# Convolution and gated product, start-up: bands without filling matmuls, two column rests in one product, weight copies ahead of loads, block 4 later

## The chip, the cores and the metric

One core of a Trainium2 chip runs the kernel. The metric is the device time of one execution in microseconds; the lower the better. Times of the profile are counted from the start of the profiled span.

## The reference

```
x:       8 sequences x 3904 tokens x 192 channels, float32
weight:  8 heads x 7 taps; softmax over the taps of each head
conv:    out[b, s, h, :] = sum over k of softmax(weight)[h, k] * x[b, s - 6 + k, h, :]   (zeros ahead of a sequence)
a = conv @ w1   (192 -> 1024)
b = conv @ w2   (192 -> 1024)
out = ((a * b) @ w3) @ w_out   (1024 -> 1024 -> 192), float32
```

The kernel multiplies w3 by w_out once (`W_sb`, 1024 x 192) and applies that product to `a * b`.

## The kernel before

The 31232 tokens form two streams (`NS = 2`), the first four sequences and the last four. The partitions hold one stream in their lower half (64 rows) and the other in their upper half. A window is 64 rows of x, of which 58 are new tokens; windows are grouped into blocks of 6, 4, 8, 10, 8, then six of 36 and one of 20.

The convolution is done on PE (TensorE): for each head a 64 x 64 band matrix is the stationary operand and x of the block the moving one (`conv`, line 291). Four groups of bands (`band`, line 256) are built at the start, from products of a diagonal with the softmaxed taps (`cprod`, line 247, on DVE), each with 28 small matmuls, and copied out of PSUM by ACT (the first two) or DVE (the last two). Between two bands stands one filling matmul on zeros, 128 columns wide (`warm(1, 128)`, line 206); five fillers of 512 columns stand at the start, and two more before the bands.

The conv's result goes to SBUF as `convo` and must then be transposed into `xT` (channels on partitions). Blocks 0 to 4 are transposed by PE (`pe_transpose`, line 340; `joint_transposes` for block 1, line 489), the later ones through DRAM (`rows`) by DMA transposes that SP queues (line 360).

Tokens of each stream are worked on in rounds of 512. In each round `first_product` makes eight tiles (ft 0 to 7) of 128 features: per tile six matmuls for w1 (`wd[0]`) and six for w2 (`wd[1]`), 64 rows each, so that both streams run side by side; then ACT copies the first result to `asb` (line 386) and DVE multiplies it with the second into `abT` (line 387). Four pairs of PSUM banks (`pairs`, `banks()`, `drained()`) go round in the order in which they were given back. `second_product` (line 415) multiplies `abT` with `W_sb`. Rounds run in groups of four: their first products, then their second products with the convs of a later block between them.

Round 0 begins before all of its 512 columns are there: block 0 gives the first 348 (`EARLY`). Tiles 0 and 1 are made for these 348 columns, and then for the other 164, when block 1 has been transposed. Tiles 2 to 7 follow at full width, with the convs of blocks 2 and 3 between them.

The weights w1 and w2 come in four parts of 256 features: part 0 by SP into `wfirst`, parts 1 to 3 by POOL's queue into the lower 64 partitions (line 172), and POOL copies each part to the upper 64 (`copy_w`, line 193). Part 1 serves tiles 2 and 3, part 2 tiles 4 and 5, part 3 tiles 6 and 7. All of this stands in program order in POOL's queue together with the loads of x (`load_x`, line 120) and of w3 (line 441, in two halves, cast to bf16 in DRAM as `w3rows`). w3 is then transposed by 16 DMA transposes on SP's queue (line 445). POOL waits for the fourteenth of them with a copy of two elements (`pace`, line 539), and only then loads x of blocks 5 and 6. Where a sequence begins inside a block, POOL zeroes the rows ahead of it after the load (line 546).

Of the kernel before, what the change touches and what calls it, by code (L numbers as in the profile page):

```python
# [9 lines left out]
BF16 = mybir.dt.bfloat16  # L10
AX = mybir.AxisListType
ALU = mybir.AluOpType
# [4 lines left out]
def kernel(  # L17
# [53 lines left out]
    def banks():  # L71
        p = free.pop(0)
        return p, pairs[:, NS * p:NS * p + NS, :]
# [4 lines left out]
    def drained(p):  # L78
        assert p not in free
        free.append(p)  # L80
# [24 lines left out]
    def load_x(b, parts=(0, 1), between=()):  # L105
        between = list(between)
        tiles = xb_of.setdefault(b, [])
        zeros_of = zero_rows.setdefault(b, [])
        for i0, n in [v for e, v in enumerate(halves_of(b)) if e in parts]:
            xb = work.tile([128, n, D], BF16, tag="xb", bufs=5, name="xb")  # L110
            w = 0
            while w < n:
                i = i0 + w
                m = min(n - w, WB - i % WB)
                at_end = i + m == NWIN
                if at_end:
                    m -= 1
                if m:
                    for r in range(NS):
                        nc.gpsimd.dma_start(out=xb[Q * r:Q * r + Q, w:w + m, :],  # L120
                                            in_=x_spans(r, i, m))
                        if between:
                            between.pop(0)()
                if i % WB == 0:
                    zeros_of += [(xb, 0, w), (xb, 1, w)]
                w += m
                if at_end:
                    nc.gpsimd.memset(xb[Q:128, w, :], 0.0)
                    t = tok(NWIN - 1) - PAD
                    nc.gpsimd.dma_start(out=xb[0:Q, w, :], in_=x_rows[t:t + Q, :])  # L130
                    nc.gpsimd.dma_start(out=xb[Q:Q + PAD + LAST, w, :],
                                        in_=x_rows[TS + t:TS + t + PAD + LAST, :])
                    w += 1
            if len(halves_of(b)) == 1:
                tiles += [(xb, 0), (xb, SIZES[b] // 2)]
            else:
                tiles.append((xb, 0))
# [8 lines left out]
    pace = const.tile([1, 2], BF16)  # L146
    tiny = const.tile([128, 1], FP32)
    ones = const.tile([128, 1], BF16)
    zeros = const.tile([128, CH], BF16)
    half = const.tile([1, 3 * Q], BF16)  # L150
    ident = const.tile([128, 128], BF16)
    diag = const.tile([128, Q + PAD], BF16)
    nc.vector.memset(tiny, 0.0)
    nc.vector.memset(ones, 1.0)
    nc.vector.memset(zeros, 0.0)  # L155
    nc.vector.memset(xb0[:, 0, :], 0.0)
    nc.vector.memset(half, 0.0)
    nc.vector.memset(half[:, Q:2 * Q], 1.0)
# [10 lines left out]
    def load_w(part):  # L169
        cs = slice(WC[part], WC[part + 1])  # L170
        for i in range(2):
            nc.gpsimd.dma_start(out=wd[i][0:Q, :, cs], in_=w_rows[i][:, :, cs])  # L172
# [18 lines left out]
    def copy_w(part, i, f):  # L191
        cs = slice(WC[part], WC[part + 1])
        f(out=wd[i][Q:128, :, cs], in_=wd[i][0:Q, :, cs])  # L193
# [3 lines left out]
    load_w(2)  # L197
    load_x(2, between=[seq((copy_w, 1, i, nc.gpsimd.tensor_copy) for i in range(2))])
    load_w(3)
    load_x(3)  # L200
    load_x(4)

    def warm(n, cols=CH):
        p, t = banks()
        for j in range(n):
            nc.tensor.matmul(t[:, j % 2, 0:cols], zeros[:, 0:128], zeros[:, 0:cols],  # L206
                             start=True, stop=True)
        drained(p)

    warm(5)  # L210

    wmax = const.tile([1, H], FP32)
    wsum = const.tile([1, H], FP32)
# [31 lines left out]
    def band(g, e):  # L245
        c = slot([128, K, Q], BF16, "cprod")
        nc.vector.tensor_tensor(
            out=c, in0=taps, in1=wsb[:, g, e].unsqueeze(2).to_broadcast([128, K, Q]),
            op=ALU.mult)
        p, bps = banks()  # L250
        for k in range(K):
            for v in range(2):
                for r in range(2):
                    rs = slice(Q * r, Q * r + Q)
                    o = Q * (r ^ v)
                    nc.tensor.matmul(bps[o:o + Q, v, 0:Q], ident[rs, rs], c[rs, k, :],
                                     start=(k == 0), stop=(k == K - 1))
        warm(1, 128)
        return p, Aband[:, g, e], bps[:, :, 0:Q]


# [13 lines left out]
    def conv(b, h0, nh, evict=None):  # L275
        n = SIZES[b] // 2
        if h0 == 0:
            convo_of[b] = work.tile([128, n, NP, NS, Q], BF16, tag="convo", bufs=2, name="convo")
        convo = convo_of[b]
        p, cps = banks()  # L280
        wd = nh * G

        def view(ps, r):
            return cps[ps, r, 0:n * wd].rearrange("p (w g) -> p w g", g=wd)

        for j in range(nh):
            h = h0 + j
            for c in range(2):
                xb, w0 = xb_of[b][c]
                for r in range(NS):  # L290
                    nc.tensor.matmul(  # L291
                        view(slice(Q * c, Q * c + Q), r)[:, :, j * G:(j + 1) * G],
                        band_of(h, r),
                        xb[Q * r:Q * r + Q, w0:w0 + n, h * G:(h + 1) * G],
                        start=True, stop=True)
        src = cps[:, :, 0:n * wd].rearrange("p r (w g) -> p r w g", g=wd)
        o, moves = 0, []
        for k, c0, m in segments(h0 * G, wd):
            moves.append((convo[:, :, k, :, c0:c0 + m].rearrange("p w r g -> p r w g"),
                          src[:, :, :, o:o + m]))  # L300
            o += m
        if h0 + nh == H:
            del xb_of[b]
        if evict == ():
            return p, moves
        for e, (dst, part) in enumerate(moves):
            f = evict or [nc.scalar.copy]
            f[e % len(f)](out=dst, in_=part)  # L308
        drained(p)
# [60 lines left out]
    def first_part(R, ft, c0, c1, ks=tuple(range(NP))):  # L370
# [18 lines left out]
        drained(qa)  # L389
        drained(qb)  # L390

    def first_tile(R):
        abT_of[R] = work.tile([128, JT, NS, CH], BF16, tag="abT", bufs=GROUP, name="abT")

# [41 lines left out]
    w3T = const.tile([128, JT, DFF], BF16)  # L436
    w3rows = dram.tile([DFF, DFF], BF16, name="w3rows")

    def load_w3():
        for j in range(0, DFF, CH):  # L440
            nc.gpsimd.dma_start(out=w3rows[j:j + CH], in_=moe_w3[j:j + CH])

    def w3_transposes(j, gts):
        for gt in gts:
# [30 lines left out]
    def move_all(p, moves, fs):  # L475
        for f, m in zip(fs, moves):
            move(f, m)
        drained(p)
# [15 lines left out]
                          src[:, :, :, 0:ST]))  # L494
        return p, moves

    move_all(*conv(0, 0, 4, ()), (V, V))
    move_all(*conv(0, 4, 4, ()), (A, A))
    for k, f in ((0, A), (2, V), (1, V)):
        p, *m = pe_transpose(0, k)  # L500
        move(f, m)
        drained(p)
    move_all(*conv(1, 0, H, ()), (A, A, V))
    first_tile(0)
    first_part(0, 0, 0, EARLY, (0, 2, 1))
    move_all(*joint_transposes(1), (A, A, V))
    first_part(0, 1, 0, EARLY)
    first_part(0, 0, EARLY, CH)
    first_part(0, 1, EARLY, CH)
    for part in (2, 3):  # L510
        for i in range(2):
            copy_w(part, i, P)
    load_w3()
    w3_transposes(0, range(JT))

    def need(R):
# [96 lines left out]
```

## Time and profile before

| | us |
|---|---|
| median of 3 runs | 525.04 (523.98 to 525.49) |
| the profiled execution | 524.21 |
| its span in the profile | 522.5 |
| PE busy | 515.0 (99% of the span) |
| DVE busy | 358.1 |
| ACT busy | 326.5 |
| POOL busy | 58.4 |

PE is TensorE's matmuls, PEld its weight loads, DVE VectorE, ACT ScalarE, POOL GpSimd, SP SyncE. A line of the time line has the start and the length in us, the engine, the line of the kernel, the operation with the tile written and the tiles read, its shape and the number of instructions merged into it; in brackets stand the idle time before it and what ended that. A merged line's length runs from the first start to the last end, so it contains the latency of the last instruction. The granted clock was 1.00 in every stage.

### The profile page before, as it was taken

What the parts mean: (1) busy time and instruction counts of PE and PEld (TensorE: products, weight loads), DVE (VectorE), ACT (ScalarE), POOL (GpSimd) and SP (SyncE); (2) the same over time, 40 slices, a digit from 0 to 9 for tenths busy, and PEclk for the clock granted to TensorE, in tenths of its full rate; (3) what the DMA queues carried; (4) which work ended last, traced back from release to release, by engine and by line L of the source; (5) the groups of instructions that cost most, each with busy time, mean ns of one, the idle gap of its engine ahead of it and who ended that gap; (6) DMA issues with size and microseconds to landing.
All of it is one profiled execution on the core that took longest, in us unless ns stands there. A gap on an engine that the chain in (4) does not pass through costs nothing.

```text
span 522.5 us, 13032 instructions
## 1 busy us (share of the span) xinstructions
PE 515.0 (99%) x5579; PEld 341.0 (65%) x5579; DVE 358.1 (69%) x348; ACT 326.5 (62%) x416; POOL 58.4 (11%) x98
## 2 busy tenths in 40 slices
PE   8899999999999999999999999999999999999997
PEld 4455688545894558945588455884558855599567
DVE  6678746799537995389953899438993299912870
ACT  6788653777437774377743777437774377735762
POOL 8501522030000200003000020001200000000000
PEclk9999999999999999999999999999999999999999
DMA  8959997699756893568745696456724532034004
GB/s 115 178 118 131 146 217 221 167 194 143 148 151 163 113 105 94 156 166 120 91 104 151 160 122 88 114 147 158 102 45 122 158 92 31 17 102 141 1 3 151
DMA packets 133421, 64.61 MB, mean 124 GB/s; under 512 B 90305, under 2 KB 132643, under 8 KB 133299
## 3 DMA queue, kind: packets, MB, share of 16 engines
q1 hardware_dynamic: 94320, 44.06, 35.5%
q0 software_dynamic: 38896, 19.62, 29.1%
q8 instruction: 43, 0.70, 0.6%
q14 instruction: 16, 0.12, 0.1%
q10 hardware_dynamic: 146, 0.10, 0.1%
HBM read 33.25 MB, written 36.52 MB: 134 GB/s over the span
## 4 chain that ended last, share of the span: by engine, by line
PE 94%; POOL 2%; DVE 1%; DMA 1%; ACT 1%; issue 0%; ACTq 0%
PE pairs L380 58%; PE pairs L415 31%; PE pairs L291 3%; DVE abT L387 1%; PE pairs L451 1%; DMA wd<-in_moe_w_dram 1%; POOL xb L120 1%; ACT asb L386 1%; PE pairs L340 0%; POOL wd L172 0%; POOL wd L193 0%; DMA wall<-in_weight_dram 0%; POOL xb L185 0%; ACT convo L308 0%; POOL xb L175 0%
## 5 line engine op out<-in xcount | busy, mean ns | idle before, releaser
L387 DVE TENSOR_TENSOR abT<-asb,pairs 128x1024 bf16<-128x1024 bf16 (+2 forms) x250 | 298.7, 1196 | 78.0 <-ACT asb L386 39.9
L380 PE MATMUL pairs<-xT,wd 64*128 64x512 bf16 (+3 forms) x3000 | 320.9, 371 | 1.8 <-POOL wd L193 0.6
L386 ACT CAST asb<-pairs 128x1024 bf16<-128x1024 f32 (+2 forms) x250 | 247.9, 992 | 69.1 <-PE pairs L380 67.2
L380 PEld LDWEIGHTS <-wd 64*128 64x128 bf16 x3000 | 163.0, 94 | 153.3 <-issue 3.1
L415 PE MATMUL pairs<-W_sb,abT 128*128 128x192 bf16 x1952 | 166.1, 246 | 0.0
L415 PEld LDWEIGHTS <-abT 128*128 128x128 bf16 x1952 | 159.6, 98 | 9.7 <-issue 9.7
L420 ACT COPY osb<-pairs 128x384 f32<-128x384 f32 x122 | 58.3, 478 | 116.0 <-PE pairs L415 116.0
L308 DVE CAST convo<-pairs 128x864 bf16<-128x864 f32 (+5 forms) x67 | 50.8, 816 | 67.3 <-PE pairs L291 63.1
L120 POOL DMA_DIRECT2D xb<-in_x_dram x42 | 32.2, 781 | 8.2 <-PE pairs L380 4.3
L568 POOL COPY pace<-abT 1x2 bf16<-1x2 bf16 x10 | 1.7, 174 | 238.6 <-DVE abT L387 238.6
L291 PE MATMUL pairs<-xb,Aband 64*64 64x432 bf16 (+5 forms) x384 | 16.9, 284 | 0.0
L291 PEld LDWEIGHTS <-Aband 64*64 64x64 bf16 x384 | 6.8, 106 | 6.8 <-issue 5.8
L308 ACT CAST convo<-pairs 128x512 bf16<-128x512 f32 (+4 forms) x15 | 8.1, 583 | 0.2
L427 POOL DMA_DIRECT2D out_dram<-osb x8 | 6.1, 758 | 18.4 <-ACT osb L420 18.4
L420 DVE COPY osb<-pairs 128x192 f32<-128x192 f32 x1 | 0.4, 358 | 11.1 <-PE pairs L415 11.1
L206 PE MATMUL pairs<-zeros 128*128 128x512 bf16 (+1 forms) x11 | 4.4, 498 | 1.3 <-DVE zeros L155 1.3
L451 PEld LDWEIGHTS <-w3T 128*128 128x128 bf16 x64 | 5.2, 98 | 0.4 <-issue 0.4
L451 PE MATMUL pairs<-wo_b,w3T 128*128 128x192 bf16 x64 | 5.5, 246 | 0.0
L193 POOL COPY wd<-wd 64x768 bf16<-64x768 bf16 x6 | 4.8, 852 | 0.5 <-DMA wd<-in_moe_w_dram 0.5
L340 PE MATMUL pairs<-ident,convo 128*128 128x128 bf16 x48 | 3.9, 219 | 0.6 <-DVE convo L460 0.5
L340 PEld LDWEIGHTS <-convo 128*128 128x128 bf16 x48 | 2.9, 97 | 2.4 <-issue 1.5
L453 ACT CAST W_sb<-pairs 128x192 bf16<-128x192 f32 x8 | 2.6, 320 | 2.8 <-PE pairs L451 2.8
(52 smaller groups left out, 40.2 us busy)
## 6 DMA issues: line engine op xcount, KB each, us to landing
out_dram<-osb SPq DMA_DIRECT2D x52, 384.0 KB
xb<-in_x_dram POOLq DMA_DIRECT2D x18, 432.0 KB, 7.8
rows<-convo SPq DMA_DIRECT2D x8, 648.0 KB
out_dram<-osb POOLq DMA_DIRECT2D x8, 384.0 KB, 4.7
w3rows<-in_moe_w_dram POOLq DMA_DIRECT2D x2, 1024.0 KB, 11.2
xb<-in_x_dram POOLq DMA_DIRECT2D x6, 240.0 KB, 6.9
rows<-convo SPq DMA_DIRECT2D x4, 324.0 KB
xT<-rows SPq DMA_TRANSPOSE x81
```

The costliest lines, as they stand in the source:

```text
L120: nc.gpsimd.dma_start(out=xb[Q * r:Q * r + Q, w:w + m, :], in_=x_spans(r, i, m))
L193: f(out=wd[i][Q:128, :, cs], in_=wd[i][0:Q, :, cs])
L291: nc.tensor.matmul(view(slice(Q * c, Q * c + Q), r)[:, :, j * G:(j + 1) * G], band_of(h, r), xb[Q * r:Q * r + Q, w0:w0 + n, h * G:(h + 1) ...
L308: f[e % len(f)](out=dst, in_=part)
L340: nc.tensor.transpose(out=tps[:, w, :], in_=convo[:, w, k].rearrange("p r g -> p (r g)"), identity=ident)
L380: nc.tensor.matmul(p[:, r, c0:c1], wd[i][rs, k, ft * 128:(ft + 1) * 128], xT[k][rs, r0 + c0:r0 + c1], start=(k == ks[0]), stop=(k == ks[-1]))
L386: nc.scalar.copy(out=asb[:, :, c0:c1], in_=pa[:, :, c0:c1])
L387: nc.vector.tensor_tensor(out=ab[:, ft, :, c0:c1], in0=asb[:, :, c0:c1], in1=pb[:, :, c0:c1], op=ALU.mult)
L415: nc.tensor.matmul(ops[:, (g - g0) * D:(g - g0) * D + D], ab[:, jt, r, g * 128:(g + 1) * 128], W_sb[:, jt, :], start=(jt == 0), stop=(jt = ...
L420: f(out=osb[:, g0:g0 + per, :].rearrange("p g d -> p (g d)"), in_=ops[:, 0:per * D])
L427: queue.dma_start(out=out[t0:t0 + ng * 128, :].rearrange("(g p) d -> p g d", p=128), in_=osb)
L451: nc.tensor.matmul(wps[:, 0, 0:D], w3T[:, gt, jt * 128:(jt + 1) * 128], wo_b[:, gt, :], start=(gt == 0), stop=(gt == JT - 1))
```

## The change

- `zeros` shrinks to 128 columns and is set first. The fillers read one column of it, broadcast to 512. Six stand at the start instead of five, and the filler after each band goes.
- POOL copies part 2 of the weights right after issuing the load of part 3, ahead of x of block 3. The first half of w3 is loaded next, then part 3 is copied, then x of block 4 is loaded, then the second half of w3. Before, x of blocks 3 and 4 was loaded first, then parts 2 and 3 were copied, then w3 was loaded.
- Each half of conv 0 is moved to SBUF by DVE and ACT together; before, DVE had the first half and ACT the second. Conv 1 is moved stream by stream (one PSUM bank each, ACT and DVE) in two moves instead of three.
- The 164 remaining columns of tiles 0 and 1 are made together by `first_rest`: both tiles side by side in one pair of banks for w1 and one for w2, one copy on ACT and one product on DVE.

```diff
-    zeros = const.tile([128, CH], BF16)
+    zeros = const.tile([128, 128], BF16)
...
+    nc.vector.memset(zeros, 0.0)
     nc.vector.memset(tiny, 0.0)
     nc.vector.memset(ones, 1.0)
-    nc.vector.memset(zeros, 0.0)
...
     load_w(3)
+    for i in range(2):
+        copy_w(2, i, nc.gpsimd.tensor_copy)
     load_x(3)
-    load_x(4)
-
-    def warm(n, cols=CH):
+
+    def warm(n):
         p, t = banks()
         for j in range(n):
-            nc.tensor.matmul(t[:, j % 2, 0:cols], zeros[:, 0:128], zeros[:, 0:cols],
+            nc.tensor.matmul(t[:, j % 2, :], zeros, zeros[:, 0:1].to_broadcast([128, CH]),
                              start=True, stop=True)
         drained(p)

-    warm(5)
+    warm(6)
...
-        warm(1, 128)
         return p, Aband[:, g, e], bps[:, :, 0:Q]
...
+        if evict == "streams":
+            assert nh == H
+            return p, [(convo[:, :, :, r, :], src[:, r].rearrange("p w (k g) -> p w k g", k=NP))
+                       for r in range(NS)]
...
+    def first_rest(R, fts, c0, c1):
+        ab = abT_of[R]
+        r0 = (R * CH) % RING
+        n, ne = c1 - c0, len(fts)
+        assert ne * n <= CH
+        pq = []
+        for i in range(2):
+            q, p = banks()
+            pq.append((q, p))
+            for e, ft in enumerate(fts):
+                for k in range(NP):
+                    for r in range(NS):
+                        rs = slice(Q * r, Q * r + Q)
+                        nc.tensor.matmul(
+                            p[:, r, e * n:e * n + n], wd[i][rs, k, ft * 128:(ft + 1) * 128],
+                            xT[k][rs, r0 + c0:r0 + c1], start=(k == 0), stop=(k == NP - 1))
+        (qa, pa), (qb, pb) = pq
+        asb = work.tile([128, NS, CH], BF16, tag="asb", bufs=3, name="asb")
+        nc.scalar.copy(out=asb[:, :, 0:ne * n], in_=pa[:, :, 0:ne * n])
+        a, b = (t[:, :, 0:ne * n].rearrange("p r (e c) -> p r e c", e=ne) for t in (asb, pb))
+        nc.vector.tensor_tensor(
+            out=ab[:, fts[0]:fts[0] + ne, :, c0:c1].rearrange("p e r c -> p r e c"),
+            in0=a, in1=b, op=ALU.mult)
+        drained(qa)
+        drained(qb)
...
-    def load_w3():
-        for j in range(0, DFF, CH):
-            nc.gpsimd.dma_start(out=w3rows[j:j + CH], in_=moe_w3[j:j + CH])
+    def load_w3(j):
+        nc.gpsimd.dma_start(out=w3rows[j:j + CH], in_=moe_w3[j:j + CH])
...
-    move_all(*conv(0, 0, 4, ()), (V, V))
-    move_all(*conv(0, 4, 4, ()), (A, A))
+    move_all(*conv(0, 0, 4, ()), (V, A))
+    move_all(*conv(0, 4, 4, ()), (A, V))
...
-    move_all(*conv(1, 0, H, ()), (A, A, V))
+    move_all(*conv(1, 0, H, "streams"), (A, V))
...
-    first_part(0, 0, EARLY, CH)
-    first_part(0, 1, EARLY, CH)
-    for part in (2, 3):
-        for i in range(2):
-            copy_w(part, i, P)
-    load_w3()
+    first_rest(0, range(2), EARLY, CH)
+    load_w3(0)
+    for i in range(2):
+        copy_w(3, i, P)
+    load_x(4)
+    load_w3(CH)
```

V, A and P are copies on DVE, ACT and POOL.

## The prediction

> **What bounds the kernel now.** I read the page first, then PE's busy time by stages, then everything PE waited for, and at last the time line of the first 20 us engine by engine.
>
> ```profile
> span 522.5 us, 13032 instructions
> ```
>
> ```profile
> 62.00:80.00 18.00, 18.00 (x226) 1.00 1.46 219
> 80.00:500.00 420.00, 419.87 (x4394) 1.00 0.60 120
> 500.00:522.50 22.50, 18.85 (x212) 1.00 0.26 89
> ```
>
> Each row is a stage: its length, PE's busy time, the granted clock, the DMA share. From 62 us on PE has no gap until the drain at the end. The change touches nothing there, so it can only shift that block, and its whole effect is the moment at which PE gets through the prologue. The waits of PE over the whole span (total, times, longest) are few; the four largest:
>
> ```profile
> PE pairs L206 <- DVE zeros L155: 1.3, 1, 1.3
> PE pairs L380 <- POOL wd L193: 0.6, 1, 0.6
> PE pairs L380 <- DVE abT L387: 0.5, 1, 0.5
> PE pairs L340 <- DVE convo L460: 0.5, 1, 0.5
> ...
> ```
>
> The change aims at all four. The profiled execution took 524.21 us, 1.71 around its span of 522.5; the median of the three timed runs is 525.04, 0.83 more. 0.3% of it is 1.58 us, about what a measurement of this kernel tells from no change: faster means below 523.46, slower above 526.62.
>
> **Bands, fillers and the first conv (net 0.1 us late).**
>
> ```profile
> 1.33 2.32 PE L206 MATMUL pairs<-zeros 128*128 128x512 bf16 x5 [1.33 <-DVE zeros L155]
> 5.41 0.29 PE L206 MATMUL pairs<-zeros 128*128 128x128 bf16 x1
> 5.63 0.59 PE L256 MATMUL pairs<-cprod,ident 64*64 64x64 bf16 x28
> 7.11 0.59 PE L256 MATMUL pairs<-cprod,ident 64*64 64x64 bf16 x28
> 7.63 0.23 PE L206 MATMUL pairs<-zeros 128*128 128x128 bf16 x1
> 7.79 0.57 PE L291 MATMUL pairs<-xb,Aband 64*64 64x72 bf16 x32
> 8.86 0.82 PE L340 MATMUL pairs<-ident,convo 128*128 128x128 bf16 x9 [0.50 <-DVE convo L460]
> 4.21 2.23 DVE L247 TENSOR_TENSOR cprod<-diag,wsb 128x448 bf16<-128x448 bf16 x4
> 8.24 0.82 DVE L460 CAST convo<-pairs 128x384 bf16<-128x384 f32 x2 [0.20 <-PE pairs L291]
> 6.56 1.67 ACT L189 CAST wd<-wfirst 64x768 bf16<-64x768 f32 x2
> 8.41 0.70 ACT L460 CAST convo<-pairs 128x192 bf16<-128x192 f32 x2 [0.17 <-PE pairs L291]
> DMA to landing us min/median/max: 3.0/3.2/3.4
> ```
>
> The smaller memset lets the warm-up start some 0.27 us before 1.33. Its sixth matmul (a step of 0.43, from five in 2.32) fills that, so the weight broadcast still goes at 3.74, when DVE has its row. A broadcast operand for the fillers I cost at nothing; six at double the step would add 2.6 us, but nothing says so.
>
> Bands now follow each other by 0.74 (5.63 to 7.11 is two). DVE delivers their factors every 0.54 or so (four in 2.23, overlapping), so without fillers the last band starts at 6.5, 0.6 earlier, and its result is there at 7.1. Conv 0 can't start at once: the last of block 0's two small loads is issued at 4.06 and lands 3.0 later (the last row, of those loads). So it starts at 7.12, 0.67 before 7.79. Its second half waits for DVE's copy of the last band, until 7.45.
>
> What follows eats this. Before, DVE moved the first half of the heads (0.82) beside ACT, which moved the second (0.70). Now each half is shared, and the built kernel's waits, listed by engine, show that two engines on one pair of banks go one after the other: ACT's first move waits for DVE's first, and DVE's second for ACT's second. The four become one chain, 0.82 + 0.70 and three handovers of 0.05, 1.67 us. It begins at 7.50, and ACT's casts, moved up 0.2 with the second band, end at 8.0 and don't stretch it: it ends at 9.17, where before the last move ended at 9.11. The transposes of k=2 and k=1 wait for that end. So the 0.67 is gone, and PE comes to the first product 0.05 to 0.15 later; I take 0.1. Conv 1's two moves, one bank each, run at once; that ends the small gap ahead of block 1's transposes and gives 0.07 back. At tile 1's first columns (11.49 before) we stand at 11.52.
>
> **The 164 columns (0.63 us won).**
>
> ```profile
> 11.49 1.84 PE L380 MATMUL pairs<-xT,wd 64*128 64x348 bf16 x30
> 13.85 3.17 PE L380 MATMUL pairs<-xT,wd 64*128 64x164 bf16 x31 [0.53 <-DVE abT L387]
> 17.64 1.58 PE L380 MATMUL pairs<-xT,wd 64*128 64x512 bf16 x11 [0.61 <-POOL wd L193]
> 11.43 0.88 DVE L387 TENSOR_TENSOR abT<-asb,pairs 128x696 bf16<-128x696 bf16 x1 [0.22 <-ACT asb L386]
> 12.92 1.93 DVE L387 TENSOR_TENSOR abT<-asb,pairs 128x696 bf16<-128x696 bf16 x3 [0.41 <-ACT asb L386]
> 15.97 2.52 DVE L387 TENSOR_TENSOR abT<-asb,pairs 128x1024 bf16<-128x1024 bf16 x2 [1.12 <-ACT asb L386]
> 12.15 1.70 ACT L386 CAST asb<-pairs 128x696 bf16<-128x696 f32 x3
> ```
>
> Counted out, the first row is 12 matmuls of 348 columns (0.074 apart) and 18 of 164 (0.035). The next holds the last 6 of 164, held 0.53 for a pair that tile 1's product on DVE frees at 13.80, and 25 of 512 (12, one tile, in 1.29). So tile 2 starts at 13.85 + 6 x 0.035 = 14.06. In the new order the 24 take two pairs instead of four. The first is freed by tile 0's product (11.43 + 0.88, shifted: 12.40), the second by block 1's last xT copy (12.6). 24 x 0.035 plus 0.1 between the halves runs from 12.45 to 13.43, and tile 2's pairs are those of tile 1's first columns, free at 12.9 and 13.8, each in time. Tile 2 at 13.43 instead of 14.06: 0.63 won. ACT's two small casts and DVE's two small products become one each (656 elements, my estimate 0.71 and 0.83, a little under the 696 of the rows), which costs no more than the pairs they replace.
>
> **Weight copies ahead of loads (another 1.0 won, 0.15 given back).**
>
> ```profile
> 12.70 1.24 POOL L172 DMA_DIRECT2D wd<-in_moe_w_dram  x2
> 13.94 2.81 POOL L120 DMA_DIRECT2D xb<-in_x_dram  x4
> 16.71 3.16 POOL L193 COPY wd<-wd 64x768 bf16<-64x768 bf16 x4
> 19.78 1.04 POOL L441 DMA_DIRECT2D w3rows<-in_moe_w_dram  x2
> 25.13 0.40 PE L291 MATMUL pairs<-xb,Aband 64*64 64x120 bf16 x16
> 36.73 0.36 PE L291 MATMUL pairs<-xb,Aband 64*64 64x96 bf16 x16
> wd<-in_moe_w_dram POOLq DMA_DIRECT2D x1, 96.0 KB, 5.5
> ```
>
> Tile 4 needs part 2's copy, which ended at 17.6 because POOL issued four loads of x first; POOL didn't wait for data there (no idle time stands at 16.71). After: two copies at 0.77, from 13.94 to 15.5. Tile 4 starts at 13.43 + 2 x 1.29 = 16.0, behind its copy; before, its second matmul went at 17.64. So the lead is 1.6. Then POOL issues x of block 3 (15.5 and 16.2 instead of 13.9 and 14.6; first used by the conv at 25.13, 23.7 now), the first half of w3 at 16.9, and part 3's copies. The second of these waits for a landing (the last row: issued at 13.3, 5.5 later, 18.8) and ends at 19.7; tile 6 wants it at 20.1.
>
> With PE earlier, what is late next is DVE: its products (1.22 each) end tile 3 at 17.85, and tile 5's first pair, wanted at 17.6, is freed by that. ACT, in order with conv 2's moves, carries 1.45 of the 1.6 through tiles 6 and 7. From there all engines shift alike. The prologue's sum: 0.1 - 0.07 - 0.63 - 1.0 + 0.15 = **-1.45 us**.
>
> **Block 4 later, w3 earlier: can the lead be kept?**
>
> ```profile
> 28.90 7.23 SPq L445 DMA_TRANSPOSE w3T<-w3rows  x2
> 33.56 21.69 SPq L445 DMA_TRANSPOSE w3T<-w3rows  x15
> 54.19 0.17 POOL L539 COPY pace<-w3T 1x2 bf16<-1x2 bf16 x1 [10.71 <-DMA w3T<-w3rows]
> w3rows<-in_moe_w_dram POOLq DMA_DIRECT2D x1, 1024.0 KB, 9.1
> 69.02 0.25 POOL L546 MEMSET xb<- 6x192 bf16 x1 [0.22 <-DMA xb<-in_x_dram]
> 69.27 0.75 PE L291 MATMUL pairs<-xb,Aband 64*64 64x432 bf16 x12
> ```
>
> This is the place where the lead can be lost. Block 5's conv starts at 69.27, and the memset that waits for its last load ends at 69.02 + 0.25 = 69.27: no slack at all. That load follows w3's transposes through the pace copy at 54.19. So a PE that is 1.45 earlier needs the w3 chain 1.45 earlier too. The first half of w3 was issued at 19.78 and landed 9.1 later; it now goes at 16.9 with block 4's 384 KB out of its way, so I expect it at 26, 2 to 3 us earlier. In the trace the first transpose then sat behind the second half of w3 (SP free for the next only at 33.56), and the rest went at some 1.4 each. If it again sits until the second half has landed, which I leave near 33 (the same bytes are ahead of it), the chain gains only 0.3; if two or three get through before, up to 4. I take 2.5, since block 4's small loads stand between the halves now. The Trainium skill, "DMA: Bandwidth & Descriptors" (Queues, rings and completion order), says that each DMA engine takes turns between its queues packet by packet; by that the transposes get through and the chain gains 2 to 4, while the 4.6 us until 33.56 shows that a turn can be long when packets are large.
>
> Block 4's x, issued at 19.7, queues behind that first half and lands by 28 to 30, my estimate; its conv, at 36.73 before, comes at 35.3.
>
> **Rivals.** *Block 5 takes it back* (0.18). The w3 chain gains only 0.3 to 1, and PE waits at 69 for the rest: 0.3 to 1.0 us won, 524.0 to 524.7. *Half clock* (0.12, the other side). The filler of 128 columns took 0.29 at 5.41 and 0.23 at 7.63, and the 512-wide step is 0.43 at first against 0.216 for a pair in tile 4 (11 in 1.58): PE runs at half speed until about 7.5, though the clock column says 1.00. Without fillers, and with a gap from 8.3 to 9.2 in place of 8.4 to 8.9, it may stay there. Up to the first product that costs 1.6 (0.9 for its 12 matmuls, the rest in convs, transposes and latencies) and cancels the gain; from there on it is a loss, and through the 164 columns it is 3.6: 527.2. Against it: the bands without fillers are denser, 0.54 instead of 0.74 apart. The Trainium skill, "TensorE: Matmul & The Clock Gate" (What's actually happening), states such a gate, at half rate until a window of about 3.4 us has been busy; by that rule 3.4 us more of half clock would cost these 1.6. The trace agrees that the first six microseconds are slow; the window itself no row shows. *The stall only moves* (0.08): part 3's landing slips by over 0.4, tile 6 waits up to 1.0, 524.6.
>
> **How the numbers follow.** Forecast (0.62): span 521.05 and 522.75 for an execution like the profiled one; from the median, 525.04 - 1.45 = 523.6. The one wait without slack, block 5's, is also one that a run 0.83 slower may have paid; with a margin of 1 us ahead of it I take half of that, 0.4, as gone: **523.2**. Bounds of the terms (bands -0.2 to +0.3, columns and copies 1.2 to 1.9) and the spread of 1.5 us among the runs give 522.0 to 524.4 for this case. Its limit, 523.46, cuts it at about 2 in 3: faster 0.42 from it and 0.02 from the first rival, slower 0.12 from half clock and 0.02 from what I don't see, the rest the same, 0.42. The range must take in the first and third rival and half clock's first step: 522.0 to 526.0.
>
> **What would show it.** Right: bands 0.54 apart, no filler, the transposes of k=2 near 9.28; tile 2 at 13.4; no wait of L380 on the copy; the first w3 transpose at 26 and the pace copy before 52.7; conv 5 near 67.8 with its memset done before. Wrong: the first product's matmuls 0.15 apart instead of 0.074 (half clock), or PE waiting at 67 to 69 for block 5.

## The result, and the profile after

| | before | changed |
|---|---|---|
| median, 22 runs each on one chip | 524.67 us (523.77 to 526.48) | 523.84 us (522.48 to 525.19) |
| the profiled execution | 524.21 | 523.71 |
| its span | 522.5 | 522.0 |

The ratio is 0.9979, with a 95% interval of 0.9970 to 0.9988: 0.83 us won. That is real, but less than the 0.3% set as the bound, so it counts as "the same". The forecast was 523.2.

The page's first line, the two stages after the prologue (length, PE's busy time, clock, DMA share, GB/s), and PE's largest waits:

```profile
span 522.0 us, 13021 instructions
...
62.00:80.00 18.00, 17.47 (x212) 1.00 1.45 223
80.00:500.00 420.00, 419.87 (x4392) 1.00 0.59 120
...
PE pairs L344 <- DVE convo L489: 1.3, 2, 0.8
PE pairs L207 <- DVE ones L155: 1.1, 1, 1.1
PE pairs L291 <- POOL xb L575: 0.5, 2, 0.4
PE pairs L384 <- DVE abT L391: 0.3, 2, 0.2
```

The long stage is as before to the hundredth. Of the four waits aimed at, the one on the weight copy is gone, and so is the one on `abT` at 13.85; two smaller ones on `abT`, of 0.15 and 0.16, stand further on, at 27.14 and 35.54. The start-up is 0.2 shorter, and the wait on the heads' moves has grown from 0.5 to 1.3. One wait is new: L291, a conv, waits for POOL's memset of `xb`. It is the one spot where the stage from 62 to 80, which had no gap, has 0.5 us of idle time.

PE's time line through the prologue, and the moves of conv 0 on DVE and ACT:

```profile
4.91 2.02 PE L257 MATMUL pairs<-cprod,ident 64*64 64x64 bf16 x112
6.88 0.71 PE L291 MATMUL pairs<-xb,Aband 64*64 64x72 bf16 x32
8.05 0.34 PE L344 MATMUL pairs<-ident,convo 128*128 128x128 bf16 x3 [0.45 <-DVE convo L489]
9.21 0.51 PE L344 MATMUL pairs<-ident,convo 128*128 128x128 bf16 x6 [0.82 <-DVE convo L489]
9.65 0.44 PE L291 MATMUL pairs<-xb,Aband 64*64 64x48 bf16 x32
10.02 1.06 PE L384 MATMUL pairs<-xT,wd 64*128 64x348 bf16 x12
...
11.45 1.06 PE L384 MATMUL pairs<-xT,wd 64*128 64x348 bf16 x12
12.39 1.07 PE L409 MATMUL pairs<-xT,wd 64*128 64x164 bf16 x24
13.28 4.07 PE L384 MATMUL pairs<-xT,wd 64*128 64x512 bf16 x36
17.27 0.36 PE L291 MATMUL pairs<-xb,Aband 64*64 64x96 bf16 x16
...
7.43 0.56 DVE L489 CAST convo<-pairs 128x384 bf16<-128x384 f32 x1 [0.15 <-PE pairs L291]
8.60 0.56 DVE L489 CAST convo<-pairs 128x384 bf16<-128x384 f32 x1 [0.61 <-ACT convo L489]
...
8.03 0.54 ACT L489 CAST convo<-pairs 128x192 bf16<-128x192 f32 x2
```

Conv 0 starts at 6.88 instead of 7.79, and nothing of that is left at the first product (10.02; 9.98 before): DVE, ACT, ACT, DVE move the heads one after the other, from 7.43 to 9.16, and PE stands idle for 0.82 until the transposes of k=2 can follow them. From there on the gain is made. The 164 columns are 24 matmuls without a gap, and tile 2 starts at 13.28 instead of 14.06. Tiles 2, 3 and 4 are 36 matmuls in one stretch, without the wait for the copy, and conv 2 starts at 17.27 instead of 19.14. DVE and ACT, busy until 17.70 and 17.74, hold tile 5 back and give up 0.18 of these 1.87 (it starts at 17.75; 19.44 before). The next rows, of after and of before, show a lead of 1.69 when PE begins `W_sb`:

```profile
59.56 5.45 PE L480 MATMUL pairs<-wo_b,w3T 128*128 128x192 bf16 x64
```

```profile
61.25 5.45 PE L451 MATMUL pairs<-wo_b,w3T 128*128 128x192 bf16 x64
...
69.96 2.24 PE L415 MATMUL pairs<-W_sb,abT 128*128 128x192 bf16 x25
```

Ten microseconds later most of it is gone in this execution. PE at block 5's conv, and POOL, in the changed kernel:

```profile
67.58 0.37 PE L291 MATMUL pairs<-xb,Aband 64*64 64x432 bf16 x2
68.31 0.34 PE L291 MATMUL pairs<-xb,Aband 64*64 64x432 bf16 x1 [0.36 <-POOL xb L575]
68.83 0.70 PE L291 MATMUL pairs<-xb,Aband 64*64 64x432 bf16 x9 [0.17 <-POOL xb L575]
69.46 0.75 PE L445 MATMUL pairs<-W_sb,abT 128*128 128x192 bf16 x7
...
68.01 0.25 POOL L575 MEMSET xb<- 6x192 bf16 x1 [3.42 <-DMA xb<-in_x_dram]
68.52 0.25 POOL L575 MEMSET xb<- 6x192 bf16 x1 [0.26 <-DMA xb<-in_x_dram]
```

Conv 5 begins 1.69 earlier than before (67.58 against 69.27), stops twice for the two memsets, and the second product behind it goes at 69.46 against 69.96. So 0.50 of 1.69 is left, and that is the difference of the two spans and of the two profiled executions (524.21 - 523.71). The memsets wait for the last loads of block 5, which are only 0.5 earlier than before. Their chain, on SP and POOL:

```profile
14.22 1.60 POOL L193 COPY wd<-wd 64x768 bf16<-64x768 bf16 x2
...
17.20 0.55 POOL L470 DMA_DIRECT2D w3rows<-in_moe_w_dram  x1
...
53.86 0.18 POOL L568 COPY pace<-w3T 1x2 bf16<-1x2 bf16 x1 [12.02 <-DMA w3T<-w3rows]
...
27.57 5.27 SPq L474 DMA_TRANSPOSE w3T<-w3rows  x1
```

The first half of w3 is issued 2.58 earlier and its first transpose starts 1.33 earlier (28.90 before), but that transpose takes 5.27, the second can start only at 32.89 (33.56 before), and the pace copy comes at 53.86 instead of 54.19: 0.33 earlier.

This is one execution. The 22 timed runs of the changed kernel fall into kinds, and the profiled one belongs to a small one of them; the first experiment tells them apart.

### The profile page after: what moved, and what is told of

Same layout as the page of the kernel before. It is cut to its first block, busy times and chain, and to the rows that moved or that the text cites. A ratio compares the mean times of both kernels' runs of the same rounds, so it can differ in the third digit from the quotient of the medians.

```text
span 522.0 us, 13021 instructions
## 1 busy us (share of the span) xinstructions
PE 514.2 (98%) x5576; PEld 340.5 (65%) x5576; DVE 358.1 (69%) x347; ACT 326.1 (62%) x414; POOL 58.6 (11%) x98
## 4 chain that ended last, share of the span: by engine, by line
PE 90%; issue 3%; DMA 2%; DVE 2%; ACT 1%; POOL 1%; ACTq 0%; POOLq 0%; DVEq 0%
PE pairs L384 56%; PE pairs L445 31%; PE pairs L291 3%; DMA xb<-in_x_dram 2%; DVE abT L391 1%; ACT asb L390 1%; PE pairs L207 1%; POOL xb L120 0%; DVE cprod L248 0%; PE pairs L344 0%; ACT convo L312 0%; DVE convo L489 0%; POOL rows L335 0%; POOL wo_b L567 0%; PE pairs L409 0%
## 5 line engine op out<-in xcount | busy, mean ns | idle before, releaser
L384 PE MATMUL pairs<-xT,wd 64*128 64x512 bf16 (+2 forms) x2976 | 319.4, 372 | 0.8 <-DVE abT L391 0.3
L291 PE MATMUL pairs<-xb,Aband 64*64 64x432 bf16 (+5 forms) x384 | 17.7, 284 | 0.5 <-POOL xb L575 0.5
L291 PEld LDWEIGHTS <-Aband 64*64 64x64 bf16 x384 | 7.2, 106 | 7.8 <-issue 6.6
L207 PE MATMUL pairs<-zeros 128*128 128x512 bf16 x8 | 3.8, 628 | 1.1 <-DVE ones L155 1.1
```

The costliest lines, as they stand in the source:

```text
L207: nc.tensor.matmul(t[:, j % 2, :], zeros, zeros[:, 0:1].to_broadcast([128, CH]), start=True, stop=True)
L291: nc.tensor.matmul(view(slice(Q * c, Q * c + Q), r)[:, :, j * G:(j + 1) * G], band_of(h, r), xb[Q * r:Q * r + Q, w0:w0 + n, h * G:(h + 1) ...
L384: nc.tensor.matmul(p[:, r, c0:c1], wd[i][rs, k, ft * 128:(ft + 1) * 128], xT[k][rs, r0 + c0:r0 + c1], start=(k == ks[0]), stop=(k == ks[-1]))
```

## The experiments

Each is an edit of the changed kernel unless it says otherwise. "Before" is the kernel before in the same series, on the same chip.

### The pace copy earlier, after and before

```diff
-    P(out=pace, in_=w3T[0:1, JT - 3, DFF - 2:DFF])
+    P(out=pace, in_=w3T[0:1, JT - 5, DFF - 2:DFF])
```

POOL waits for the twelfth transpose instead of the fourteenth, and asks for block 5 earlier: by 2.6 us in the kernel before (the pace copy at 51.60), by 3.6 in the changed kernel (50.27).

> The changed kernel, but POOL's pace copy reads w3's twelfth transpose instead of the fourteenth, so that x of blocks 5 and 6 is asked for some 2.6 us earlier; nothing else moves. Theory 'block 5': in the changed kernel PE came to block 5's conv at 67.58, 1.69 earlier than before, and lost 1.19 of that waiting for block 5's x, whose load starts only 0.33 earlier. With the load earlier the wait goes, the conv's four groups run from 67.6 without a gap, and the span falls by 1.2, from 522.0 to 520.8; the median comes to about 522.6. Rival 'additive': the wait is replaced by another one (w3's last transposes now compete with x, so W_sb at 59.6 or block 6 comes late), and the span stays at 521.8 to 522.2.

> The kernel before with the same earlier pace copy and nothing else. The prediction took 0.4 us of the median of before for a late block 5 in slower executions. If that is so, this kernel is 0.3 to 0.8 us faster than the kernel before. If block 5 came just in time in most executions (a wait of 0.04 in the profile), it changes by less than 0.2, and the 0.4 was wrong.

In the changed kernel: 523.73 against 524.95 of before, 0.9974 (0.9962 to 0.9985). In the kernel before: 524.63, 1.0004 (0.9990 to 1.0018). So in the kernel before there is no sign of a gain: the 0.4 us that the prediction took off its median, for a late block 5 in longer executions, is not seen. In the changed kernel the expected 522.6 was missed, although the profile shows conv 5 without a wait. In the profiled execution the reason is in the prologue. PE's busy time in three stretches, and PE's time line, of this kernel:

```profile
6.49:9.90 3.41, 1.98 (x96) 1.00 1.10 122
9.90:13.31 3.41, 3.41 (x54) 0.50 1.07 115
13.31:16.72 3.41, 3.41 (x52) 1.00 1.08 113
...
10.21 1.92 PE L384 MATMUL pairs<-xT,wd 64*128 64x348 bf16 x12
12.06 0.82 PE L518 MATMUL pairs<-ident,convo 128*128 128x128 bf16 x6
```

Each of the first three rows is a stretch, with its length, PE's busy time and the granted clock. PE ran at half clock (0.50) for 3.41 us, behind a stretch of the same length in which it was busy for 1.98 us, 58%: the two gaps at the moves of conv 0 lie in it. The 12 matmuls of the first product take 1.92 instead of 1.06. `W_sb` starts at 61.06, 1.50 later than in the profile of the changed kernel.

The column falls at 9.90 and rises 3.41 later; I call such a stretch a window. It falls again behind the last matmul, at 521.90, which is 512.0 us or 150 windows of 3.413 behind the first fall; in the profile of the split columns below the two falls, at 10.08 and 522.08, lie as far apart. So the fall at the end tells where the boundaries are in a profile with no fall in the prologue. In that of the changed kernel it comes at 520.35, and counted back in the same steps the boundaries lie elsewhere:

```profile
4.93:8.34 3.41, 2.59 (x148) 1.00 1.25 134
8.34:11.76 3.42, 2.60 (x62) 1.00 1.02 118
```

The two gaps are split between two windows of 76% each, and the clock stays whole. The profile of the split columns below has a third case: 52% (1.78 us), and then half clock.

The timed runs carry a mean clock each. One window at half clock is 0.5 x 3.41 of some 520, which makes 0.997. Of the 22 runs of the changed kernel 14 had 0.997 or less (median 523.90), and the other eight a median of 522.6: about 1.3 us. Of these eight, five lie at 522.48 to 522.61 and three at 523.71 to 524.04, the profiled execution among the three. The five have spans of 520.8 to 520.9, which is the whole lead of 1.69: block 5 can have taken nothing of note from them. So the wait at block 5 in the profile belongs to a minority, and the median, 523.84, is a time of the half-clock kind.

With the early pace copy it was 5 of 12 (524.0). The other seven have a median of 523.4, no better than the eight of the changed kernel (522.6, on a chip where before is 0.28 faster). What held some of them up no profile shows. One candidate is the rival named above: the last transposes of w3 now compete with x, as the last profile of this section has it. Of the kernel before, in the series of this section, 4 of 90 had a half-clock window. Its full-clock runs spread as well, from 523.8 to 525.7 in this series, and the early pace copy leaves that as it is (523.7 to 525.7); the cause is not known.

### One part alone undone

*The 164 columns tile by tile* (`first_part` for tile 0 and tile 1 in place of `first_rest`):

> The changed kernel with the 164 columns of tiles 0 and 1 made tile by tile again, as before. The step itself is worth 0.6 us at the end of the prologue by the prediction: W_sb's product starts at 60.2 instead of 59.56. Theory 'block 5': the load of block 5 sets when the conv at 67.6 ends, so undoing this costs nothing: 522.0 in the span, the same median as the changed kernel. Rival 'additive': the span grows by 0.6 to 522.6.

524.71, 0.9984 (0.9973 to 0.9996). Compared at like clocks: at full clock 523.4 against 522.6, with a half-clock window 524.8 against 523.9. That is 0.8 to 0.9 for the joint product, though from two chips, whose runs of before differ by 0.28. By the ratio to the early-pace kernel of this chip (0.9974) it is 0.5, with overlapping intervals; against that kernel at like clocks it is 0.7 with a half-clock window and nothing at full clock (523.4 both). So the size is uncertain. My expectation that block 5 would hide the step was wrong: the median rose, and in the profile, one with a half-clock window, PE comes to block 5 at 70.13 and doesn't wait.

*Conv 0's moves as before, with the early pace copy:*

```diff
-    move_all(*conv(0, 0, 4, ()), (V, A))
-    move_all(*conv(0, 4, 4, ()), (A, V))
+    move_all(*conv(0, 0, 4, ()), (V, V))
+    move_all(*conv(0, 4, 4, ()), (A, A))
```

> The first kernel of this group (earlier pace copy) with conv 0's moves as before: DVE takes the first half of the heads, ACT the second; conv 1 stays stream by stream. If the chain of four moves one after the other is what ate the bands' 0.7 us, the transposes of k=2 start near 8.8 instead of 9.21 and the span falls by 0.3 to 0.4 against the first kernel, to 520.4. If the split moves were the better ones, it rises by 0.1 to 0.3.

522.87, 0.9971 (0.9956 to 0.9987); 3 of 12 runs with a half-clock window. PE's time line:

```profile
9.37 0.44 PE L291 MATMUL pairs<-xb,Aband 64*64 64x48 bf16 x31 [0.21 <-DMA xb<-in_x_dram]
9.74 1.06 PE L384 MATMUL pairs<-xT,wd 64*128 64x348 bf16 x12
```

The gap before the transposes of k=2 is gone. The first product starts at 9.74 instead of 10.02, not earlier, because conv 1 now waits for block 1's load. So the shared moves cost 0.28, and the load would take the rest. By the ratios (0.9971 and 0.9974) the two kernels can't be told apart. This profile, at full clock and with the early pace copy, is also the one that keeps its whole lead:

```profile
67.34 0.74 PE L291 MATMUL pairs<-xb,Aband 64*64 64x432 bf16 x12
68.01 2.81 PE L445 MATMUL pairs<-W_sb,abT 128*128 128x192 bf16 x32
```

`W_sb` starts at 59.31, 1.94 ahead of the kernel before, the second product behind conv 5 is 1.95 ahead (68.01 against 69.96), and the span is 520.6 against 522.5.

### Fillers in the gaps

If the gaps cause the half clock, matmuls without a use in them must take it away, without shortening any wait. One filler of 512 columns goes ahead of block 0's transposes and two after those of k=0:

```diff
+    pf, tf = banks()
+    fill(tf, 1)
     for k, f in ((0, A), (2, V), (1, V)):
...
+        if k == 0:
+            fill(tf, 2)
+    drained(pf)
```

> The changed kernel with three filling matmuls (512 columns on zeros) in the two gaps in which PE waits for conv 0's moves: one ahead of block 0's transposes, two between k=0 and k=2. Nothing else changes. In two of the profiles so far the clock column fell to 0.50 for one stretch of 3.41 us that followed a stretch with PE 52% or 58% busy; stretches with 76% kept 1.00. Theory 'gap clock': most executions of the changed kernel (14 of 22 show a mean clock of 0.993 to 0.997) lose about 1.4 us by this. With the gaps filled hardly any should show such a clock. But then PE is always as early as in its profile and meets block 5's late x, so the gain is partly taken back there: 523.0 to 523.7, against 523.8 for the changed kernel. Rival 'fillers only delay': they push k=2's transposes, W_sb's product starts after 59.7 in a profile at full clock and the time rises by 0.2 to 0.4.

> The same fillers and the earlier pace copy (w3's twelfth transpose). If the two losses, the half clock in the prologue and block 5's late x, take turns in hiding each other, either mend alone gives little and both together give all: a span of 520.8 and a median of 522.4 to 522.7, in nearly all executions. If either is not a cause, the median stays at 523.3 to 523.9.

The first has the pace copy as changed, the second has it early. With the two kernels above this is a square:

| median; ratio to before (interval); runs with a half-clock window | pace as changed | pace early |
|---|---|---|
| gaps empty | 523.84; 0.9979 (0.9970-0.9988); 14 of 22 | 523.73; 0.9974 (0.9962-0.9985); 5 of 12 |
| gaps filled | 523.06; 0.9970 (0.9960-0.9980); 0 of 12 | 522.95; 0.9969 (0.9957-0.9981); 0 of 5 |

The times alone don't part the four, since the intervals overlap; the median with both, 522.95, is a little above the 522.4 to 522.7 that I expected. The clock does part them: over all the kernels with fillers in the gaps none of 67 runs had such a window, over the four without them 29 of 58. With the gaps filled the kernel gains 0.30% with either pace copy, some 1.6 us, about what the prologue's sum had promised. PE's time line and waits with the gaps filled and the pace copy late:

```profile
8.18 0.60 PE L528 MATMUL pairs<-zeros 128*128 128x512 bf16 x2
9.17 0.51 PE L344 MATMUL pairs<-ident,convo 128*128 128x128 bf16 x6 [0.39 <-DVE convo L489]
...
PE pairs L291 <- POOL xb L585: 0.9, 2, 0.7
```

The transposes start where they did (9.17), the half clock is gone, and PE, which is early again, waits 0.9 at block 5. Its conv 5 begins at 67.85 and the second product behind it at 70.11: 2.26 where an undisturbed conv takes 0.67 (67.94 to 68.61 with the early pace copy). In the profiles, then, the time of the pace copy goes with what becomes of the lead. With the copy at 53.7 to 53.9 a lead of 1.69 shrank to 0.50 and one of 1.42 to nothing (a span of 522.7). With the copy at 51.1 to 51.3 leads of 1.33 and 1.94 came through whole.

But the profile with filled gaps and the late copy is the slowest of its twelve runs (524.36). Nine of the others lie at 522.7 to 523.2, with spans of 521.0 to 521.5, so they kept most of the lead with the same late copy. Block 5 takes 1.2 to 1.6 in some executions, and nothing of note in most.

### POOL's old order with the rest

The kernel with filled gaps and the early pace copy, with loads and copies in the order of before: x of blocks 3 and 4, then both copies, then w3.

> Both mends, but POOL's order as before the change: x of blocks 3 and 4 ahead of the copies of parts 2 and 3, then both halves of w3. The prediction's term for this is 1.0 us, less 0.15 given back: PE should wait for the copy at tile 4 again (0.6 idle by the profile, 1.0 in matmul starts), and the time should be 0.9 us over the kernel with both mends: 523.4. If the copies were not what held tile 4, the time stays at 522.5.

525.09, 1.0001 (0.9991 to 1.0010): 2.1 us lost. PE's time line and waits:

```profile
17.46 1.58 PE L383 MATMUL pairs<-xT,wd 64*128 64x512 bf16 x11 [0.99 <-POOL wd L193]
...
PE pairs L479 <- DMA w3T<-w3rows: 1.2, 1, 1.2
PE pairs L383 <- POOL wd L193: 1.0, 1, 1.0
```

The wait for the copy is back, longer than before (1.0 for 0.6), since the columns still bring PE there early: by tile 7 PE is 1.5 later (23.49 against 22.00). The rest is a wait that the prediction did not price: the w3 chain starts later (first transpose at 29.75), the early pace copy sends block 5's loads beside its last transposes, and `W_sb` waits 1.2 for those. This profile is the slowest of its eleven runs (526.25), so that wait can't be counted whole in the 2.1.

### Fillers after the bands again

With the gaps filled and the early pace copy, the 128-column filler after each band as before:

> The kernel with both mends (gap fillers, earlier pace copy) and the 128-column filler after each band put back as before the change. The prediction said that the bands' earlier end (0.67 us at conv 0) is eaten whole by the chain of shared moves. With the fillers back conv 0 starts at 7.7 and the chain runs after that: if band fillers and moves are each worth what was priced, the first product starts 0.6 later (10.7 against 10.07) and the span grows by 0.6 over the kernel with both mends. If the bands' end does not matter there, it starts at 10.1 and nothing changes.

523.53 against 524.57, 0.9978 (0.9968 to 0.9989). Conv 0 starts at 7.87 instead of 6.96, the first product at 11.10 instead of 10.07 and `W_sb` at 60.64 instead of 59.92. The band fillers thus cost 0.7 in the profile and some 0.5 by the ratios (0.9978 against 0.9969, two chips, overlapping intervals); the prediction gave them 0.67.

```profile
9.36 1.06 PE L529 MATMUL pairs<-zeros 128*128 128x512 bf16 x2
```

These are the two fillers behind the transposes of k=0. They took 0.60 with filled gaps above; at 1.06 they run about as slowly as the two fillers ahead of the bands (1.03), though the clock column says 1.00. So the column, and with it the mean clock of a run, shows a fall from full speed and not a slow start, and the counts of half-clock windows are counts of such falls. In this execution the slow start lasts until past 10 us. It explains some 0.1 of the 1.03 at the first product (3.23 from conv 0 to there, instead of 3.11); the rest is conv 0's later start.

### How far it goes

Four more put the pieces together:

- the moves of conv 0 as before, with one filler ahead of block 0's transposes, one behind them, and the early pace copy;
- the same with both halves of w3 issued together, ahead of part 3's copies and block 4's x;
- the gap fillers with the halves together in the same place and the pace copy as changed;
- the first of these with the pace copy one transpose earlier still.

> Earlier pace copy, conv 0's moves as before the change (DVE the first half, ACT the second), and one filling matmul ahead of block 0's transposes and one behind them. The moves were worth 0.25 us at W_sb's start (59.31 against 59.56), with less of a gap to fill. Expected: 0.2 to 0.3 under the kernel with both mends, a span of 520.5 and a median of 522.2.

> Earlier pace copy, conv 0's moves as before the change, a filler ahead of and behind block 0's transposes, and w3's two halves issued one right after the other, ahead of the copies of part 3 and of block 4's x. In every trace the first w3 transpose could not be followed by the next before w3's second half had landed (32.9 to 33.6); issued next to the first half it should land near 32, so that the chain gains 1 to 1.5 us and block 5's x comes before PE wants it at 67.3: a span of 520.4 and a median of 522.1, in nearly all executions. If block 4's x then comes after 34.9, PE waits at its conv and the span is 0.3 to 1 longer.

> The kernel with the gap fillers alone (pace copy on w3's fourteenth transpose, as in the changed kernel) and w3's two halves issued next to each other. Theory 'stuck transpose': the pace copy comes 1 to 1.6 us earlier than the 53.7 to 53.9 of the kernels with block 4's x between the halves, and block 5's wait shrinks to under 0.7 (it was 1.56 in the profile with the gap fillers alone). Rival: the chain is set by SP's own issue times after the first transpose was issued at 27.2, and the pace copy stays at 53.7.

> The changed kernel with conv 0's moves as before, fillers in the two gaps around block 0's transposes, and the pace copy on the eleventh w3 transpose (three earlier than in the changed kernel). With the twelfth the profile had lost 0.7 us at block 5, whose last load landed at 67.67 for a conv due at 67.29. Theory (block 5 and the clock are all that holds the lead): one transpose is 1.3 us, the last load lands near 66.4, conv 5 runs straight from 67.3, W_sb near 59.3, no execution below a mean clock of 0.998: 522.5 us, ratio near 0.996. Rival (the load's landing hangs on the other DMA traffic and not on the pace copy): still 0.3 to 0.7 lost at block 5, 523.2.

| | median | before | ratio (interval) |
|---|---|---|---|
| old moves, fillers, pace on the 12th | 523.35 | 525.04 | 0.9969 (0.9957-0.9981) |
| the same, halves of w3 together | 522.80 | 524.57 | 0.9966 (0.9954-0.9979) |
| gap fillers, halves together, pace on the 14th | 523.00 | 524.57 | 0.9968 (0.9957-0.9979) |
| old moves, fillers, pace on the 11th | 522.25 | 525.06 | 0.9956 (0.9941-0.9971) |

The first two missed the medians that I expected, 522.2 and 522.1. In the profile of the first conv 5 waits 0.25 for the memset, and half of its runs lie between 523.5 and 524.2; no profile shows why. The third is the test of the stuck transpose. SP and POOL with the halves together:

```profile
27.03 1.23 SPq L474 DMA_TRANSPOSE w3T<-w3rows  x1
27.03 2.52 SPq L474 DMA_TRANSPOSE w3T<-w3rows  x2
...
51.10 0.18 POOL L578 COPY pace<-w3T 1x2 bf16<-1x2 bf16 x1 [9.05 <-DMA w3T<-w3rows]
```

The first transpose takes 1.23 instead of 5.27 and the pace copy is 2.8 earlier than in the changed kernel (53.86) with the same rule for it; conv 5 has no wait, and a lead of 1.47 at `W_sb` is whole in the span (521.0). Issuing the halves together is not enough by itself: in the kernel before and in the one with POOL's old order they are issued together too, behind x of blocks 3 and 4, and there the first transpose took 4.61 and 4.69. What the two kernels with the short transpose share is that block 4's x goes behind both halves. Nor is it always the first transpose that sits. In the profile with the early pace copy alone the first, at 25.20, was followed by the second at 27.30, and that one took 4.66. In the second kernel of the table, POOL being later there, block 4's x comes late instead: conv 4 waits 0.7 at 36.16.

The last is the fastest, 2.3 us under its before by the ratio, and 6 of its 9 runs lie at 522.05 to 522.35. Its profiled execution, 523.82, is one of the other three and shows the limit of that lever. PE's and POOL's time lines:

```profile
64.08 2.24 PE L480 MATMUL pairs<-wo_b,w3T 128*128 128x192 bf16 x25 [1.42 <-DMA w3T<-w3rows]
...
50.12 0.17 POOL L577 COPY pace<-w3T 1x2 bf16<-1x2 bf16 x1 [8.57 <-DMA w3T<-w3rows]
...
68.25 0.25 POOL L584 MEMSET xb<- 6x192 bf16 x1 [0.23 <-DMA xb<-in_x_dram]
```

The pace copy is 1.46 earlier than on the twelfth (51.58), but block 5's memset no earlier (67.72 there), and the last transposes of w3, with these loads beside them, come late for `W_sb` by 1.4. The 66.4 that I expected for the last load was wrong in this execution. The time of asking is not all, either: with the early pace copy alone block 5 was asked for at nearly the same time (a copy at 50.27), and its last memset stood at 63.82.

## Why the prediction was right or wrong

**The prologue: right in each step, 0.24 low in the sum.** Bands 0.54 apart: yes. A chain of four moves of 1.67 us: 1.73. Transposes of k=2 at 9.28: 9.21. Tile 1's columns at 11.52: 11.45. Tile 2 at 13.43: 13.28. Lead at the copy 1.6, of which 0.15 is given back: 1.87 and 0.18. The sum was -1.45, the profile has -1.69. That the bands' gain is eaten by the shared moves holds from both sides: band fillers put back cost 0.5 to 0.7, old moves put back win 0.28 before block 1's load becomes the limit.

**The terms don't stand alone.** Costed apart, the columns were 0.63 and the copies 1.0. Undone alone, the columns cost 0.5 to 0.9 by most comparisons, and POOL's old order cost 2.1 (with another wait at `W_sb`). Without the copies' new place, the columns' gain only lengthens the wait for the copy (0.6 to 1.0).

**"Can the lead be kept?": here the forecast failed in the profiled execution.** The term is the w3 chain, taken as 2.5 us earlier, with bounds of 0.3 and 4. The profile has 0.33. The step that failed is the choice between the bounds: that block 4's small loads between the halves would let two or three transposes through. The first half landed at 27.6 and not at 26, and the first transpose sat for 5.27 until the second half was nearly in. The rival *Block 5 takes it back* (0.18) is what the profiled execution did, with 0.5 us won as it priced, 0.3 to 1.0. It is not what most runs did: the five fastest kept the whole lead by their spans, and in the 14 with a half-clock window it was mostly gone before block 5, if they are like the early-pace profile, which lost 1.50 by `W_sb`. The Trainium skill, "DMA: Bandwidth & Descriptors" (Queues, rings and completion order), by whose packet-by-packet turns the chain would gain 2 to 4, doesn't fit the changed kernel; it fits the one with the halves together ahead of block 4's x, where four transposes of 1.23 to 1.26 went while the second half (landed at 31.4) was under way. It doesn't fit the kernel before, where the halves stand together too and the first transpose took 4.61.

**Half clock: named as a rival at 0.12, and it acted in 14 of 22 runs.** The price was near (1.6 through the first product; 1.3 to 1.5 measured), and so was the place (the gap from 8.3 to 9.2). Wrong were its chance and the end that went with it, 527.2 and slower: the clock does not stay low from the start on, it falls for one window of 3.41 us and comes back, and the 1.3 is paid out of the gain, not on top of before. Against it the forecast had counted that the bands are denser; what decided was the two gaps behind them, and where a window's boundary falls. The row that I named for it, first-product matmuls 0.15 apart, is there in the early-pace kernel (12 in 1.92). The Trainium skill, "TensorE: Matmul & The Clock Gate" (What's actually happening), gives a free-running window of 3413 ns, and the traces agree on its length. By its rule against gaps longer than about 3 us (Why this matters for your kernels) these gaps, 0.45 to 0.61 and 0.82, would be harmless; the traces have half clock behind windows that were 52% and 58% busy, and none behind 76%.

**The median.** 0.4 us were taken off for a block 5 late in slower executions. The kernel before with an early pace copy showed no such gain (1.0004), so that term had nothing behind it. Without it the forecast would have been 523.6, near the 523.84 measured, but by luck. The gain measured is 0.83, against a before of 524.67 on the same chip, which itself lies 0.46 above the profiled execution of before. Of the 22 runs, fourteen have a larger prologue gain (1.69) less 1.3 to 1.5 at the clock (two of them lost twice that, with a mean clock of 0.993); three have times like the profile's, which lost 1.2 at block 5; only five keep the prologue's gain whole.

**Open.** How busy a window must be to keep the clock: between 58% and 76% by the profile's busy time, if that is what counts. Why one transpose sits for 4 to 6 us where x of block 4 goes ahead of or between the halves of w3, and none does where it goes behind both: the runs show that it is so, not what holds it, and none shows that the size of packets, which the prediction named, has to do with it. Why block 5's x is late in some executions of a kernel and in time in others. Why even with filled gaps some executions lose 1 to 2 us; in one of them it was w3's last transposes.

## What to carry to other kernels

A lead won early is worth what the next timed arrival allows: follow it to the first place where an engine waits for a transfer of its own schedule, and move that transfer too, before counting the lead as won. When filling matmuls go, look at PE's busy share over a few microseconds, not at the single gap: several short gaps in one clock window cost more than the fillers did. Put two parts of a change back together and one by one, since waits in a row share their price. And sort the timed runs into kinds before reading the one profile, which may belong to the smallest of them.

## What the hardware showed that I had not expected

- Two gaps, 0.54 or 0.61 and 0.82 us long, within one 3.41-us window (52% or 58% busy) were followed by half of TensorE's clock for the next 3.41 us, which cost 1.3 to 1.5 us here. The profile whose window boundary falls between the gaps (76% busy on both sides) kept its clock, and one program has executions of both kinds.
- TensorE's slow start does not show in the clock column: two fillers of 512 columns took 1.06 us at a column of 1.00 in one profile, and 0.60 in another.
- One DMA transpose took 5.27 us beside a large copy from DRAM to DRAM in one order of the loads, and 1.23 us in another.
- Asking for x 1.5 us earlier did not land it earlier in one execution (68.25 against 67.72), and the last transposes were late too; in another execution x asked for at nearly the same time was there by 63.82.
